# Retention followed by a gated cosine MLP: the order of the opening blocks, of the weight and block loads, and of the transposes against the stores

## The chip, the cores and the metric

The kernel runs on one core of a Trainium2 chip. The metric is the device time in microseconds (us) of one execution. Three runs of the kernel before gave 314.37, 314.63 and 315.67 us, so the median is 314.63 us. A profiled execution, from which every duration below comes, took 315.27 us; its span from the first to the last instruction was 313.6 us, and 1.7 us lie around the span.

Engines carry the profile's names: PE (TensorE matmul), PEld (its weight loads), DVE (VectorE), ACT (ScalarE), POOL (GpSimd) and SP (SyncE, which here only issues transfers). A name with q (SPq, POOLq) is the sequencer of that engine.

## The reference

Two layers follow each other. The first is a retention: for 8 batches and 8 heads, q, k and v have 576 rows of 64 numbers.

```python
scores = scale * np.matmul(q, k.transpose(0, 1, 3, 2))
Dmat = np.where(rel >= 0, gamma[:, None, None] ** rel[None, :, :], 0.0)
ret = scores * Dmat[None, :, :, :]
attn_out = np.matmul(ret, v)
```

The output is laid out as x with 4608 tokens of 512 numbers, and the second layer is

```python
h = x @ w_in            # 512 -> 2048
g = h * np.cos(h)
out = g @ w_out         # 2048 -> 512
```

## The kernel before

**Tiles.** The 4608 tokens are cut into 18 blocks of 256 (number j), and two blocks make a stage of 512 tokens (number n, 0 to 8). The retention of a block is computed in chunks of 128 tokens with a state that is carried from chunk to chunk.

**One block of retention.** `load` (L134 for pairs of rows, L148 for the later blocks) fetches q, k and v on SP's queue into buffers of which there are three for each name (`AHEAD = 3`). `scaled` (L165) multiplies q and k with the decay and rounds them into `qks`; `round_v` (L176, with L180 to L183 for chunks that cross the end of a batch) rounds v into `vb`. The transpose to `qkT` is done on PE for blocks 0 to 3 (`transpose_pe`, L209, with an evacuation of PSUM at L214) and by a DMA transpose on SP's queue for later ones (`transpose_dma`, L196). `scores` (L238, L267) multiplies, and a mask on DVE gives `ret` (L247, L277). `scores_y` (L299, L307) is the same in halves, for block 3. `sums_of` (L331) gives the chunk's own state; DVE adds it to the running one (L348 to L361) and ACT rounds it into `sb` (L371). `out_own` (L387) and `out_carried` (L419) accumulate the block's output in one PSUM tile `ov`, which is evacuated as `xT` (L442, or L444 on ACT and L445 on DVE in halves).

**The layers of a stage.** `mm1` (L457) makes eight blocks of h, each 1024 numbers wide in PSUM: 16 matmuls of 256 columns in stages 0 and 1, and 8 of 512 in the others. ACT takes the cosine (L465, a sine with a bias of half pi), and DVE multiplies it with h into `gT` (L466). The second layer of stage 0 is 64 plain matmuls (L865) with other work inserted after given numbers of them (the list `todo`). From stage 1 on it is a product of the Strassen kind: seven products (L557) of sums of quarters of g (`g_sum`, L504, on DVE and, for sum 7 from stage 2 on, on POOL) and of w_out (`w_sums`, L484), put together in `ot` (L583, L587) and stored (`stored_rows`, L573, on SP's queue).

**Order.** It is written out by hand (`manual_schedule`): each engine runs its instructions in the order of the program, and SP and POOL issue transfers in that order too. A transfer of a later line can't overtake an instruction that waits ahead of it on the same queue. `load_w_in` and `load_w_out` (L657, L663) are issued on POOL, in four pieces each. `load(..., gate=x)` makes the first transfer of a block wait until the weight transfer x has landed. In the kernel before, block 2 waits for the first piece of w_out (`w_dma[4]`), and block 3 for the third (`w_dma[6]`). `step` prepares the next block: four `scaled` on POOL, the DMA transpose, `round_v`, and the load of one more block; `steps_to(j)` does so until block j-1 is prepared. `stored(u)`, called after store u of a stage, calls it:

```python
if n == 1:
    steps_to({3: 7}.get(u, 0))
elif n == 2:
    steps_to({0: 8, 1: 9, 2: 10, 3: 11}[u])
else:
    steps_to({0: 2 * n + 6, 1: 2 * n + 7}.get(u, 0))
```

**PSUM.** There are three tags of two banks, a, b and m, and two of one, n and st. The blocks of stage 0 take them in the order m, b, m, a, b, m, a, b (`banks_of`); a block waits until the tile that had its tag before has been read.

Of the kernel before, what the change touches and what calls it, by code (L numbers as in the profile page):

```python
# [8 lines left out]
F32 = mybir.dt.float32  # L9
# [3 lines left out]
ACTF = mybir.ActivationFunctionType  # L13
# [4 lines left out]
def kernel(  # L18
# [51 lines left out]
    lng = consts.tile([P, H], F32)  # L70
    ln_scale = consts.tile([P, 1], F32)
    half_pi = consts.tile([P, 1], F32)
    qpos_i = consts.tile([P, PERQ, 2, H], I32)
    qpos = consts.tile([P, PERQ, 2, H], F32)
    kpos_i = consts.tile([P, PERK, H], I32)
# [354 lines left out]
    def x_of(j):  # L430
        n = j // 2
        if ("x", n) not in tiles:
            tiles["x", n] = xp.tile([P, DG, W], BF16, tag="xT", name="xT")
        return tiles["x", n][:, :, j % 2 * BK : j % 2 * BK + BK]
# [12 lines left out]
    def mm1(n, et, c0, w, bank, inside={}):  # L447
        if ("g", n) not in tiles:
            tiles["g", n] = gp.tile([P, ET, W], BF16, tag="gT", name="gT")
        gT, xT = tiles["g", n], tiles["x", n]  # L450
        m = 1024 // w
        ps = psum.tile([P, m, w], F32, tag=bank, name="h")
        for j in range(m):
            if j in inside:
                inside[j]()
            for dg in range(DG):
                nc.tensor.matmul(  # L457
                    ps[:, j, :],
                    lhsT=w_in_sb[:, dg, (et + j) * P : (et + j + 1) * P],
                    rhs=xT[:, dg, c0 : c0 + w],  # L460
                    start=(dg == 0),
                    stop=(dg == DG - 1),
                )
        cosh = cosp.tile([P, m, w], F32, tag="cosh", name="cosh")
        nc.scalar.activation(cosh, ps, ACTF.Sin, bias=half_pi, scale=1.0)  # L465
        nc.vector.tensor_mul(gT[:, et : et + m, c0 : c0 + w], ps, cosh)  # L466
# [169 lines left out]
    def load_next(**kw):  # L636
        nonlocal loaded
        if loaded < NB:
            load(loaded, **kw)
            loaded += 1  # L640
# [15 lines left out]
    def load_w_in(e0):  # L656
        return nc.gpsimd.dma_start(  # L657
            w_in_sb[:, :, e0 : e0 + 512],
            moe_w_in[:, e0 : e0 + 512].rearrange("(dg p) e -> p dg e", p=P),
        )  # L660
# [80 lines left out]
    scaled(nc.vector, 0, "q", 1)  # L741
    transpose_pe(0, "q", "n", act, (0,))
    transpose_pe(0, "q", "st", vec, (1,))
    round_v(0)
    w_dma = [load_w_in(0)]
    scaled(nc.gpsimd, 1, "k", 0)
    scaled(nc.gpsimd, 1, "k", 1)
    w_dma += [load_w_in(512)]
    for masked in scores(0, "ab", idle=2):
        masked()  # L750
    sums_of(0, "st")()()
    scaled(nc.vector, 1, "q", 0)
    scaled(nc.vector, 1, "q", 1)
    transpose_pe(1, "k", "n", act, (0,))
    ps0 = psum.tile([P, DG, BK], F32, tag="m", name="ov")
    out_own(0, ps0)
    transpose_pe(1, "k", "st", act, (1,))
    out_carried(0, ps0)
    act(x_of(0)[:, :2], ps0[:, :2])
    vec(x_of(0)[:, 2:], ps0[:, 2:])  # L760
    transpose_pe(1, "q", "n", act, (0,))
    transpose_pe(1, "q", "st", vec, (1,))
    round_v(1)
    w_dma += [load_w_in(e) for e in (1024, 1536)] + [load_w_out(0)]
    m1 = scores(1, "ab", idle=2)
    m1[0]()
    add1 = sums_of(1, "st")
    m1[1]()
    add1()()
    load_next(names="kqv", gate=w_dma[4])  # L770
    nc.gpsimd.tensor_copy(mask_mix, mask_p)
    nc.gpsimd.tensor_copy(mask_cmix, mask_c)
    for r in range(2):
# [3 lines left out]
    for name in "kq":  # L777
        for y in range(2):
            scaled(nc.gpsimd, 2, name, y)
        w_dma += [load_w_out(4 + "kq".index(name) * 4)]  # L780
    round_v(2)
    w_dma += [load_w_out(12)]
    load_next(names="kqv", gate=w_dma[6])
    load_next()
    prep(3)
    round_v(3)
# [19 lines left out]
    blocks_of[0][1:3] = blocks_of[0][2:0:-1]  # L806
    banks_of = {0: "mbmabmab", 1: "abmamabm"}

    later = {}

    def block2_scores():
        masks = scores(2, "ab")
        masks[0]()
        add = sums_of(2, "a")
        masks[1]()
        add()()

    def block3_sums():
        sums_of(3, "n")()()
# [1 line left out]
    for n in range(NT):  # L821
        blocks = blocks_of.get(n) or [(e + k * E2, 0, W) for e in range(0, E2, 2) for k in range(2)]
        for i, (et, c0, cw) in enumerate(blocks):
            inside = {
                (0, 0): {2: lambda: outputs(1, "a", act, vec)},
                (1, 1): {1: lambda: scores_y(3, 0, ("n", "st"))},
                (1, 2): {1: lambda: scores_y(3, 1, ("n", "st"))},
                (1, 3): {2: block3_sums},
            }.get((n, i), {})
            mm1(n, et, c0, cw, banks_of.get(n, "abmabmab")[i], inside)  # L830
            if (n, i) == (1, 1):
                steps_to(5)
            if (n, i) == (1, 3):
                outputs(3, "b", act, vec)
                for e in range(0, E2, 2):
                    w_sums(7, e, e + 2)
            if (n, i) == (1, 5):
                steps_to(6)
            if n:
                sums_after(n, i)  # L840
        if n == 0:
            gT = tiles["g", n]
            two = psum.tile([P, 2, DM], F32, tag="m", name="o")
            pss = [psum.tile([P, DM], F32, tag=t, name="o") for t in ("n", "st")]
            pss += [two[:, k] for k in range(2)]
            todo = [
                (12, lambda: transpose_pe(2, "k", "a", act)),
                (18, lambda: transpose_pe(2, "q", "b", act)),
                (26, block2_scores),
                (46, lambda: outputs(2, "b", act, vec)),  # L850
                (56, lambda: transpose_pe(3, "k", "a", act)),
                (62, lambda: transpose_pe(3, "q", "b", act)),
            ]
            todo += [
                (at, lambda x=x, e=e: w_sums(x, e, e + 4))
                for at, x, e in (
                    (4, 5, 0), (10, 5, 4), (50, 6, 0), (53, 6, 4), (57, 4, 0), (60, 4, 4)
                )
            ]
            todo.sort(key=lambda u: u[0])  # L860
            for done in range(4 * ET):
                while todo and todo[0][0] <= done:
                    todo.pop(0)[1]()
                e, t = divmod(done, 4)
                nc.tensor.matmul(  # L865
                    pss[t],
                    lhsT=gT[:, e, t * P : (t + 1) * P],
                    rhs=w_out_sb[:, e, :],
                    start=(e == 0),
                    stop=(e == ET - 1),  # L870
                )
            for t in range(4):
                ot = op.tile([P, 1, DM], F32, tag="abcd"[t], name="ot")
                (act, vec)[t % 2](ot[:, 0], pss[t])
                stored_rows(t * P, 0, DM, ot)
            load_next()
            load_next()
            continue

        a, b = 2 * n + 2, 2 * n + 3  # L880

        def first_unit(flush, pend):
            def then():
                late_sums(n, (5, 6))
                flush()
                outputs(a, "m")

            intro(b, "ab", "st", pend, then)

        def second_unit(flush, pend):  # L890
            def then():
                flush()
                outputs(b, "m")

            if b + 1 < NB:
                intro(b + 1, "ab", "st", pend, then)
            else:
                then()

        def only_intro(flush, pend):  # L900
            flush()
            if n == 1:
                late_sums(n, (7,))
            intro(a, "ab", "m")
            if n == 1:
                pend.append(lambda: late_sums(n, (3,)))

        def mid_unit(flush, pend):
            def then():
                flush()  # L910
                outputs(a, "m")

            intro(b, "ab", "st", pend, then)

        def end_unit(flush, pend):
            def then():
                flush()
                outputs(b, "m")

            if n > 1:  # L920
                intro(b + 1, "ba", "a", pend, then)
            else:
                then()

        if n in (1, 2):
            at = {6: only_intro, 5: mid_unit, 3: end_unit}
        else:
            at = {2: first_unit, 5: second_unit} if n < last else {}

        def stored(u):  # L930
            if n == 1:
                steps_to({3: 7}.get(u, 0))
            elif n == 2:
                steps_to({0: 8, 1: 9, 2: 10, 3: 11}[u])
            else:
                steps_to({0: 2 * n + 6, 1: 2 * n + 7}.get(u, 0))

        mm2_seven(n, at, stored)


# [28 lines left out]
```

## Time and profile before

| what | value |
|---|---|
| median of 3 runs | 314.63 us |
| profiled execution | 315.27 us |
| its span | 313.6 us |
| PE busy | 288.6 us (92%) |
| DVE busy | 220.1 us (70%) |
| POOL busy | 152.6 us (49%) |
| ACT busy | 136.3 us (43%) |
| mean granted clock of PE | 0.966 |
| PE idle for anything it waited for, after 136 us | none |

In the timeline a row has its start, its duration, the engine, the source line, the operation with output and inputs, and the number of instructions; in brackets stands the idle time of the engine ahead of it and what ended it. In the chain of waits each row is a piece of the chain that ended last. In the list of waits a row has the waiting line, what it waited for, the sum in us, the number of waits and the longest. In the windows a row has its stretch, its length, the busy time of PE, PEld, DVE, ACT and POOL (with instructions), the granted clock of PE (1.00 is full), the busy share of the DMA engines and the rate in GB/s.

### The profile page before, as it was taken

What the parts mean: (1) busy time and instruction counts of PE and PEld (TensorE: products, weight loads), DVE (VectorE), ACT (ScalarE), POOL (GpSimd) and SP (SyncE); (2) the same over time, 40 slices, a digit from 0 to 9 for tenths busy, and PEclk for the clock granted to TensorE, in tenths of its full rate; (3) what the DMA queues carried; (4) which work ended last, traced back from release to release, by engine and by line L of the source; (5) the groups of instructions that cost most, each with busy time, mean ns of one, the idle gap of its engine ahead of it and who ended that gap; (6) DMA issues with size and microseconds to landing.
All of it is one profiled execution on the core that took longest, in us unless ns stands there. A gap on an engine that the chain in (4) does not pass through costs nothing.

```text
span 313.6 us, 7653 instructions
## 1 busy us (share of the span) xinstructions
PE 288.6 (92%) x3258; PEld 197.4 (63%) x3258; DVE 220.1 (70%) x270; ACT 136.3 (43%) x158; POOL 152.6 (49%) x182
## 2 busy tenths in 40 slices
PE   7787989869999997599999999999999999999991
PEld 3566745758874585344884587468648855874680
DVE  5755754856985997349965977797689669836931
ACT  3535532544344623046435633663364446326520
POOL 7910936996301399813972493269247113102300
PEclk9799999998999999589999999999999999999997
DMA  7996989999998829999999819964700530121014
GB/s 228 275 190 162 167 154 270 225 221 243 243 255 199 202 65 248 239 186 278 208 246 214 203 40 239 249 148 103 167 3 2 119 84 0 36 69 35 2 33 100
DMA packets 128930, 49.78 MB, mean 159 GB/s; under 512 B 89344, under 2 KB 128384, under 8 KB 128896
## 3 DMA queue, kind: packets, MB, share of 16 engines
q1 hardware_dynamic: 124672, 45.10, 60.5%
q0 software_dynamic: 4224, 4.19, 8.6%
q8 instruction: 25, 0.41, 0.5%
q14 instruction: 9, 0.07, 0.1%
HBM read 36.70 MB, written 9.44 MB: 147 GB/s over the span
## 4 chain that ended last, share of the span: by engine, by line
PE 70%; DMA 9%; POOL 8%; DVE 5%; issue 3%; ACT 1%; SPq 1%; DVEq 0%; POOLq 0%; ACTq 0%
PE h L457 33%; PE o L557 28%; POOL qks L165 4%; DMA w_out_sb<-in_moe_w_out_dram 4%; DMA fk<-in_k_dram 3%; PE o L865 3%; DVE gT L466 2%; DMA fv<-in_v_dram 2%; PE ov L387 2%; PE sc L267 2%; PE st L331 1%; ACT cosh L465 1%; POOL vb L176 1%; DMA qkT<-qks 1%; PE ov L419 1%
## 5 line engine op out<-in xcount | busy, mean ns | idle before, releaser
L457 PE MATMUL h<-xT,w_in_sb 128*128 128x512 bf16 (+1 forms) x704 | 129.8, 345 | 3.8 <-DVE gT L466 1.6
L466 DVE TENSOR_TENSOR gT<-h,cosh 128x1024 bf16<-128x1024 f32 x72 | 87.9, 1222 | 39.0 <-ACT cosh L465 38.8
L465 ACT ACTIVATE cosh<-h,half_pi 128x1024 f32<-128x1024 f32 x72 | 80.1, 1114 | 79.7 <-PE h L457 79.7
L457 PEld LDWEIGHTS <-w_in_sb 128*128 128x128 bf16 x704 | 69.6, 99 | 60.4 <-issue 5.2
L504 POOL TENSOR_TENSOR gs<-gT 128x512 bf16<-128x512 bf16 x28 | 35.8, 1279 | 116.6 <-DVE gT L466 116.6
L557 PEld LDWEIGHTS <-gs 128*128 128x128 bf16 x520 | 50.2, 99 | 7.3 <-issue 0.2
L557 PEld LDWEIGHTS <-gT 128*128 128x128 bf16 x384 | 37.1, 98 | 6.2
L165 POOL TENSOR_TENSOR qks<-fq,gq 128x512 bf16<-128x512 f32 x32 | 35.5, 1131 | 3.2 <-DMA fq<-in_q_dram 3.1
L583 DVE TENSOR_TENSOR ot<-ot,o 128x512 f32<-128x512 f32 x39 | 25.9, 680 | 14.0 <-ACT ot L587 7.9
L587 ACT COPY ot<-o 128x512 f32<-128x512 f32 x32 | 18.7, 586 | 38.7 <-PE o L557 38.7
L277 DVE TENSOR_TENSOR ret<-sc,mask_c 128x1024 bf16<-128x1024 f32 x25 | 29.8, 1213 | 4.8 <-PE sc L267 4.8
L557 PE MATMUL o<-w_out_sb,gs 128*128 128x256 bf16 (+1 forms) x264 | 32.3, 278 | 0.0
L165 POOL TENSOR_TENSOR qks<-fk,gkc 128x512 bf16<-128x512 f32 x28 | 31.3, 1137 | 0.0
L557 PE MATMUL o<-ws,gs 128*128 128x256 bf16 x256 | 30.7, 273 | 0.0
L557 PE MATMUL o<-w_out_sb,gT 128*128 128x256 bf16 x256 | 30.1, 273 | 0.0
L176 POOL CAST vb<-fv 128x512 bf16<-128x512 f32 x36 | 22.5, 653 | 1.4 <-DMA fv<-in_v_dram 1.4
L442 ACT CAST xT<-ov 128x1024 bf16<-128x1024 f32 x14 | 14.2, 1012 | 12.2 <-PE ov L419 12.2
L371 ACT CAST sb<-s 128x512 bf16<-128x512 f32 (+1 forms) x18 | 10.3, 574 | 18.2 <-DVE s L359 7.7
L387 PE MATMUL ov<-ret,vb 128*64 128x128 bf16 (+1 forms) x352 | 12.9, 229 | 3.9 <-DVE ret L277 1.9
L165 POOL TENSOR_TENSOR qks<-fk,gkp 128x512 bf16<-128x512 f32 x6 | 6.1, 1043 | 21.0 <-DMA fk<-in_k_dram 20.9
L361 DVE TENSOR_TENSOR s<-st,s 128x256 f32<-128x256 f32 x18 | 7.6, 423 | 11.7 <-PE st L331 11.4
L504 DVE TENSOR_TENSOR gs<-gT 128x512 bf16<-128x512 bf16 (+1 forms) x25 | 15.4, 615 | 0.4
(81 smaller groups left out, 216.8 us busy)
## 6 DMA issues: line engine op xcount, KB each, us to landing
out_dram<-ot SPq DMA_DIRECT2D x70, 128.0 KB, 2.5
fk<-in_k_dram SPq DMA_DIRECT2D x25, 256.0 KB, 4.8
fv<-in_v_dram SPq DMA_DIRECT2D x25, 256.0 KB, 4.6
fq<-in_q_dram SPq DMA_DIRECT2D x12, 512.0 KB, 4.3
w_in_sb<-in_moe_w_in_dram POOLq DMA_DIRECT2D x4, 512.0 KB, 6.9
w_out_sb<-in_moe_w_out_dram POOLq DMA_DIRECT2D x4, 512.0 KB, 6.4
fk<-in_k_dram SPq DMA_DIRECT2D x3, 512.0 KB, 6.0
fv<-in_v_dram SPq DMA_DIRECT2D x3, 512.0 KB, 6.0
```

What stands on the lines that cost most here:

```text
L165: return eng.tensor_tensor(out=dst.rearrange("p b a d -> p a b d"), in0=src.rearrange("p (a b) d -> p a b d", a=2), in1=by.rearrange("p (a ...
L176: runs[y](vb[:, y], f[:, :, y, :] if j < NP_B else f[:, y])
L277: nc.vector.tensor_tensor(out=ret[:, k].rearrange("p a b i -> p (a b) i"), in0=pss[k].rearrange("p a b i -> p (a b) i"), in1=mask.unsqueez ...
L387: nc.tensor.matmul(ps[h % 2 * D : h % 2 * D + D, h // 2, c.c0 : c.c0 + P], lhsT=vb[c.rows, y, h, :], rhs=rhs, start=part not in begun, sto ...
L442: evac(x, ps)
L457: nc.tensor.matmul(ps[:, j, :], lhsT=w_in_sb[:, dg, (et + j) * P : (et + j + 1) * P], rhs=xT[:, dg, c0 : c0 + w], start=(dg == 0), stop=(d ...
L465: nc.scalar.activation(cosh, ps, ACTF.Sin, bias=half_pi, scale=1.0)
L466: nc.vector.tensor_mul(gT[:, et : et + m, c0 : c0 + w], ps, cosh)
L504: eng.tensor_tensor(out=tiles["gs", n, x][:, e : e + step], in0=a[:, e : e + step], in1=b[:, e : e + step], op=op_,)
L557: nc.tensor.matmul(dst[i], lhsT=lhs[:, e, j * P : (j + 1) * P], rhs=rhs[:, e, c0:c1], start=(fresh and e == 0 and (i == 0 or len(parts) > 2)),
L583: return lambda: nc.vector.tensor_tensor(out=out_, in0=in0, in1=in1, op=ALU.add)
L587: nc.scalar.copy(t, tiles["all", x])
```

## The change

The change only moves work, with two additions: a sine of one number for each partition, and one constant tile for its result.

1. **Opening, blocks 0 and 1.** One half of v of block 0 is rounded on ACT in place of POOL, and both halves of block 1 too. The scaling of half 0 of q of block 1 goes from DVE to POOL, ahead of the second to fourth pieces of w_in. The evacuations of three transposes of block 1 go from ACT to DVE. `xT` of block 0 is evacuated by ACT alone. The scores of block 1 lose the two warming matmuls ahead of them, and both masks come after the state sums. The tiny sine is issued on ACT ahead of the scores.
2. **Block 1's output.** `outputs(1)` stood inside the first block of layer one. Now `out_own(1)` comes behind that whole block, `out_carried(1)` after a quarter of the second block, and ACT evacuates it ahead of the second block's cosine.
3. **Weights and loads.** The first two pieces of w_out are issued straight after w_in. Block 2's loads wait for the fourth piece of w_in, and block 3's for the second piece of w_out.
4. **Second layer of stage 0.** Block 2's scores come after 24 matmuls (26 before) and its state sums after 34, no longer straight behind the scores. Block 3's transposes come after 52 and 59 (56 and 62 before). `outputs(2)` and `outputs(3)` are evacuated by ACT alone.
5. **Steps.** One of the two loads behind stage 0 goes. Block 4 is prepared after block (1, 0) of layer one, block 5 after (1, 4), block 6 after store 0 of stage 1, block 7 after store 3, and block 8 after block (2, 2) of layer one, ahead of POOL's sums of stage 2. On SP's queue the transposes of blocks 4 to 8 so stand ahead of loads and stores that they stood behind.

```diff
+        if (n, et, c0) == (0, 4, 0):
+            nc.scalar.copy(x_of(1), ps1[0])
         cosh = cosp.tile([P, m, w], F32, tag="cosh", name="cosh")
...
-    round_v(0)
+    round_v(0, (nc.gpsimd.tensor_copy, act))
     w_dma = [load_w_in(0)]
-    scaled(nc.gpsimd, 1, "k", 0)
-    scaled(nc.gpsimd, 1, "k", 1)
-    w_dma += [load_w_in(512)]
     for masked in scores(0, "ab", idle=2):
         masked()
     sums_of(0, "st")()()
-    scaled(nc.vector, 1, "q", 0)
+    scaled(nc.gpsimd, 1, "k", 0)
+    transpose_pe(1, "k", "n", act, (0,))
+    scaled(nc.gpsimd, 1, "k", 1)
+    scaled(nc.gpsimd, 1, "q", 0)
     scaled(nc.vector, 1, "q", 1)
-    transpose_pe(1, "k", "n", act, (0,))
+    w_dma += [load_w_in(e) for e in (512, 1024, 1536)] + [load_w_out(e) for e in (0, 4)]
+    load_next(names="kqv", gate=w_dma[3])
+    round_v(1, (act, act))
     ps0 = psum.tile([P, DG, BK], F32, tag="m", name="ov")
     out_own(0, ps0)
-    transpose_pe(1, "k", "st", act, (1,))
+    transpose_pe(1, "k", "st", vec, (1,))
     out_carried(0, ps0)
-    act(x_of(0)[:, :2], ps0[:, :2])
-    vec(x_of(0)[:, 2:], ps0[:, 2:])
-    transpose_pe(1, "q", "n", act, (0,))
+    act(x_of(0), ps0)
+    transpose_pe(1, "q", "n", vec, (0,))
     transpose_pe(1, "q", "st", vec, (1,))
-    round_v(1)
-    w_dma += [load_w_in(e) for e in (1024, 1536)] + [load_w_out(0)]
-    m1 = scores(1, "ab", idle=2)
-    m1[0]()
+    nc.scalar.activation(sine, half_pi, ACTF.Sin, bias=0.0, scale=1.0)
+    masks1 = scores(1, "ab")
     add1 = sums_of(1, "st")
-    m1[1]()
+    for masked in masks1:
+        masked()
     add1()()
-    load_next(names="kqv", gate=w_dma[4])
...
-        w_dma += [load_w_out(4 + "kq".index(name) * 4)]
+        w_dma += [load_w_out(8 + "kq".index(name) * 4)]
     round_v(2)
-    w_dma += [load_w_out(12)]
-    load_next(names="kqv", gate=w_dma[6])
+    load_next(names="kqv", gate=w_dma[5])
     load_next()
...
-                (0, 0): {2: lambda: outputs(1, "a", act, vec)},
+                (0, 1): {1: block1_carried},
...
-            if (n, i) == (1, 1):
+            if (n, i) == (0, 0):
+                block1_own()
+            if (n, i) == (1, 0):
                 steps_to(5)
             if (n, i) == (1, 3):
-                outputs(3, "b", act, vec)
+                outputs(3, "b")
...
-            if (n, i) == (1, 5):
+            if (n, i) == (1, 4):
                 steps_to(6)
+            if (n, i) == (2, 2):
+                steps_to(9)
...
-                (26, block2_scores),
-                (46, lambda: outputs(2, "b", act, vec)),
-                (56, lambda: transpose_pe(3, "k", "a", act)),
-                (62, lambda: transpose_pe(3, "q", "b", act)),
+                (24, block2_scores),
+                (34, block2_sums),
+                (46, lambda: outputs(2, "b")),
+                (52, lambda: transpose_pe(3, "k", "a", act)),
+                (59, lambda: transpose_pe(3, "q", "b", act)),
...
             load_next()
-            load_next()
...
             if n == 1:
-                steps_to({3: 7}.get(u, 0))
-            elif n == 2:
-                steps_to({0: 8, 1: 9, 2: 10, 3: 11}[u])
+                steps_to({0: 7, 3: 8}.get(u, 0))
             else:
-                steps_to({0: 2 * n + 6, 1: 2 * n + 7}.get(u, 0))
+                steps_to({0: 2 * n + 6, 2: 2 * n + 7}.get(u, 0))
```

The new helpers `block1_own` and `block1_carried` call `out_own(1)` into a PSUM tile of tag a and `out_carried(1)` into the same; `block2_sums` calls `sums_of(2, "a")`.

## Prediction

> **What bounds the kernel now.** I read the list of PE's waits first, because PE is busy 92% of the span and after 136 us waits for nothing at all. Every time that a change of order can win therefore lies ahead of that point, in waits of PE and in the clock that PE loses through them. (Better than 0.5%, some 1.6 us, is what a measurement of this kernel can tell from no change.) PE's waits in the whole span, those that matter here:
>
> ```profile
> PE sc L267 <- DMA qkT<-qks: 4.5, 1, 4.5
> PE ov L387 <- DVE ret L277: 1.9, 2, 1.4
> PE h L457 <- DVE gT L466: 1.6, 1, 1.6
> ...
> PE st L331 <- DVE ret L247: 1.4, 1, 1.4
> ...
> PE h L457 <- ACT xT L444: 1.1, 1, 1.1
> PE h L457 <- DVE xT L445: 1.0, 1, 1.0
> ```
>
> Then the windows, cut where the granted clock changes (the columns are length, busy PE, PEld, DVE, ACT, POOL, clock, DMA share, GB/s):
>
> ```profile
> 22.78:26.19 3.41, 1.76 (x17) 1.44 (x15) 2.00 (x2) 2.37 (x3) 0.00 (x0) 1.00 0.91 150
> ...
> 67.15:70.56 3.41, 1.34 (x10) 1.02 (x10) 1.82 (x2) 1.01 (x2) 3.41 (x5) 0.95 0.84 189
> 70.56:73.97 3.41, 3.41 (x19) 2.45 (x18) 0.58 (x1) 1.11 (x1) 1.01 (x2) 0.54 1.06 258
> ...
> 121.76:125.17 3.41, 1.38 (x42) 0.94 (x40) 2.75 (x4) 0.55 (x1) 3.41 (x5) 0.96 1.06 240
> 125.17:135.41 10.24, 6.33 (x54) 4.00 (x55) 3.04 (x3) 0.76 (x2) 7.05 (x9) 0.51 0.98 232
> ```
>
> A stretch of 3.4 us with 1.34 or 1.38 us of PE work is followed by half the clock, for 3.4 us and for 10.2 us; one with 1.76 us of work is not. So a wait costs itself and, past a point between these, half of the PE work that follows. Last, the chain of waits up to the longest of them:
>
> ```profile
> 109.39 0.19 POOL gs L504
> ...
> 111.62 3.67 POOL qks L165 x3
> ...
> 117.90 4.06 DMA fk<-in_k_dram
> 121.96 3.20 POOL qks L165 x4
> 125.16 3.88 DMA qkT<-qks
> ...
> 129.08 1.07 PE sc L267 x29
> ```
>
> POOL's sums of g (L504) hold up the preparation of block 7, whose transpose stands ahead of block 10's load and block 8's transpose on SP's queue; PE waits for that last one from 124.6 to 129.1 us.
>
> **Step 1, the opening: -2.8 us.** In the timeline, block (0, 0) of layer one does 8 matmuls at 17.58 us and then PE waits 0.85 us for block 1's mask and 0.24 us for `sb`. Its cosine comes only at 23.04 us, behind half an `xT` (21.14 us, 0.59 us) and the table load:
>
> ```profile
> 21.74 1.28 ACT L465 ACT_TABLE_LOAD   x1
> 23.04 2.12 ACT L465 ACTIVATE cosh<-h,half_pi 128x1024 f32<-128x1024 f32 x2
> 24.18 2.35 DVE L466 TENSOR_TENSOR gT<-h,cosh 128x1024 bf16<-128x1024 f32 x2 [1.73 <-ACT cosh L465]
> 25.46 1.25 PE L457 MATMUL h<-xT,w_in_sb 128*128 128x256 bf16 x10 [1.65 <-DVE gT L466]
> ```
>
> The third block starts at 25.46 us, when `gT` has freed bank m. After the change I lay the same rows in the new order. POOL: half of v (0.59), the issue of w_in (0.95), then three `qks` of 1.02 each end at about 12.6. DVE: masks of block 0 to 12.2, one `qks` of 1.24, three evacuations of 0.42 as PE delivers them, the last at about 15.8. Scores of block 1 at 16.0 (16.39 before), masks (2.35) to 19.0, state add (0.68) to 19.7, `sb` (0.62) to 20.3. On PE, state sums (0.8) and all 16 matmuls of (0, 0) fill 16.6 to 19.0, then own, a quarter of (0, 1), carried at 20.35, the rest until 22.0. On ACT, in its order: `sb` to 20.3, cosine (1.11) to 21.4, `xT` of block 1 (1.01, row L442) to 22.4; the table load (1.28) ran at about 15.6 to 16.9, where ACT waits for `sb`. DVE's `gT` (1.23) ends at 22.7, and the third block starts there: 25.5 - 22.7 = 2.8 us. The w_in piece for block (0, 1) landed at 12.05 + 6.4 = 18.45 us; it is issued 0.55 us later now, and even 19.0 is ahead of its use at 19.7 (if not, the wait is the excess). Block 1's v on ACT needs `fv`, landed at 12.4, and costs 2 x 0.6 ahead of `xT` of block 0 at 14.5: covered. The six blocks that follow take 10.5 us as before, at PE's pace.
>
> **Step 2, weights and loads: 0.** Second piece of w_out: five pieces landed 2.5 to 3.0 us apart on the same queue, so a sixth lands at about 26.55 + 2.6 = 29.2 us when alone; it is used at about 36.5. Block 2's load is gated 2.5 us earlier (24.05 for 26.55). Even if sharing gives that back, POOL's rows of before (k ready at 33.6, q at 36.4, `v_mix` at 41.7) meet PE's new wants (35.7, 37.4, 41.8). Block 3's load starts at 29 to 33 us (41.8 before); its k and q, ready at 50.9 and 54.2 before, are wanted at 47.7 and 49.5, so 5 of the 9 us are needed. The third and fourth pieces of w_out landed at 41.8 and 48.6; wanted at 41.5 and 46.9. They are issued behind two `scaled` each, 3 to 7 us earlier, and now meet loads 3 and 4. Ends: nothing, or what rival B says. I take nothing, the nearest row being the 7.0 us (5.5 to 5.7 without) of the piece that met load 3 before.
>
> The Trainium skill (DMA: Bandwidth & Descriptors, "Issuing engines are not separate DMA queues") says that transfers of all issuing engines interleave on the same 16 DMA engines. By that, early loads would slow the weights, and this part could cost rather than be free; the 7.0 us beside 5.5 is the only trace of it here, and by it the sum would lose 1.5 us at most if a piece had no slack.
>
> **Step 3, second layer of stage 0: -1.4 us.** State sums straight behind the scores took bank a and waited 1.37 us for the mask. Ten matmuls of 0.21 us now stand between, 2.1 us, with two masks of 1.2 us: the first has freed the bank. The layer took 35.94 to 55.5; it now runs from about 33.1 to 51.3.
>
> **Step 4, block 3's output: -0.6 us, and -1.7 us of clock.** PE waited 1.13 us for ACT's half of `xT` and 1.00 for DVE's, which stood behind `gT`. One evacuation by ACT (1.01) behind the cosine that ends at 67.69 gives 68.7: 62 matmuls start at 68.97 for 69.60. PE now works about 3.41 - 1.66 = 1.75 us of that stretch; the row with 1.76 kept the clock, the one with 1.34 lost it. I take the nearer: 3.41 / 2 = 1.7 us are not lost.
>
> The Trainium skill (TensorE: Matmul & The Clock Gate, "HAM oscillation") allows PE gaps up to 3.4 us. The trace differs: the clock fell after waits of 1.13 and 1.00 us. By the rule the clock is safe in the new order with more to spare; by the row it is close. Both give the same 1.7 us, with different certainty.
>
> **Step 5, transposes ahead: -4.5 us, and -3.1 us of clock.** I walk SP's queue with durations of before: eight stores of block 0 (5.1) from about 51.9; load 5 (6.2) to 63.2; transpose 4 (2.4); load 6 (6.9) to 72.5; transpose 5 (3.0); load 7 (5.7) to 81; two store halves (1.3), transpose 6 (2.5), load 8 (5.9) to 91, landed at 95; six stores (5), transpose 7 at 96, load 9 (5), transpose 8 at 103, landed at 107. Wanted, in the new time: transpose 4 at 75 (lands 69), 5 at 82 (79), 6 at 105.6 (88), 7 at 112.8 (102), 8 at 118. So the 4.5 us go with 11 us to spare. POOL prepares 4 at once behind 3, so its queue carries them: block 8 from 91 to 97 (four of 1.13, two of 0.65, the last behind the landing). Behind that stand the sums of g, four of 1.28, wanted by product 7 at 116.35 - 6.5 = 109.8: ready at about 103. Six stores behind load 8 free their `ot` tiles at about 97, wanted again at 104. What is late next is PE itself, and the 1.4 us wait for `ret` at 123.8, which stays; a stretch with it alone has some 2 us of work, above 1.76. So the 10.24 us at half clock, of which 6.3 were PE work, give back 3.1 us.
>
> **Sum.** 2.8 + 1.4 + 0.6 + 1.7 + 4.5 + 3.1 = 14.1 us. The profiled execution took 315.27 us, so 301.2 us. It lies 0.64 us above the median of the runs, which are 1.3 us apart; by the median it would be 300.5. I keep **301.2**.
>
> **Rivals.**
> - *A, clock not won.* The cold stretch of step 4 stays (1.7), or one more comes in the opening, whose two warming matmuls (0.77 us at 15.3) are gone (1.7). For it: 1.75 us is at the edge. Against: 1.76 kept the clock. 302.9 to 304.6.
> - *B, weights late.* Loads 3 and 4 push the last pieces of w_out behind them. Begun at 31 us, the two loads (1.57 MB each, 4.5 us at the 346 GB/s of the first loads, some 6 for the later, small rows) and the two pieces (2.6 each, three with interference) would end at 47 to 49; the last 16 matmuls and inserts (5 us) then end at 54.5 where 51.3 was hoped for, with up to 1.7 of clock: 3 to 5 us, 304 to 306.
> - *C, the transpose isn't won.* Block 8's load or POOL is late enough that PE waits as before. Only steps 1, 3 and 4 remain: 315.27 - 6.5 = 308.8. Against: 11 us of slack.
> - *D, slower.* On POOL, block 8's preparation now stands ahead of the sums of g. If load 8 lands at t, the sums end at about t + 8, and product 7 waits from t = 102 on, 1 us for each us, plus half clock. From t = 116 on, the gain of 14 is eaten: 317 and more. Against: load 8 landed at about 96.5 even in the old order.
>
> **How the numbers follow.** Forecast 0.58, A 0.17, B 0.10, C 0.07, D 0.05, better by up to 2 us 0.03 (PE's two waits at 60 us, 0.8, and most of the 1.66 of step 4 go too: 299.0). The range 299.0 to 306.0 holds all but C and D, somewhat over 8 in 10. Faster: all but D and a part of the unknown, 0.92; same 0.02; slower 0.06.
>
> **What would show it.** Step 1: third block of L457 near 22.7 us, the table load before 18 us. Step 2: no wait of L865 for w_out. Step 3: no wait of L331 for `ret`. Step 4: one wait of L457 for `xT`, below 1.7 us, full clock behind it. Step 5: no wait of L267 for a DMA, and full clock from the opening to the end. Wrong, if PE waits for w_out or for `gs`, or if the clock falls at a place where it did not before.

## The result, and the profile after

The changed kernel takes 314.17 us (median of 17 runs, 309.97 to 318.22) where the kernel before took 315.25 beside it: a ratio of 0.993, with a 95% interval of 0.990 to 0.996. Here and below, times are medians of all runs, while ratios leave out the slow runs, those over 1.5% above the fastest of their kernel (7 of these 17, the profiled one among them, and 2 of the 4 of e9). The forecast was 301.2 with a range from 299.0 to 306.0, so it was wrong by 13 us, and the time lies outside the range. The profiled execution took 315.17 us (span 313.5), 0.1 less than that of before. A second profile of the same kernel, of 314.48 us (e1 below), shows the same waits, each longer or shorter by up to 1 us, and is given where it matters.

The lines of the changed kernel are numbered 1 to 13 higher: L457 of before is L458, L557 is L560, L865 is L878. PE's waits, to be laid beside the list of before:

```profile
PE o L560 <- POOL qks L166: 3.4, 1, 3.4
PE o L878 <- DMA w_out_sb<-in_moe_w_out_dram: 2.2, 1, 2.2
PE tr L210 <- POOL qks L166: 2.1, 3, 1.2
PE ov L388 <- DVE ret L278: 1.9, 2, 1.4
...
PE h L458 <- ACT xT L443: 1.6, 1, 1.6
```

Every wait that the change was aimed at is gone: 4.5 us of L267 for a transpose, 1.6 of L457 for `gT`, 1.4 of L331 for `ret`, and the two for halves of `xT` have become one. But new ones stand in their place, for w_out, for `qks`, and one of 3.4 us in the second layer. The start of each stage on PE tells where the gain was won and given back:

| start of | before | forecast | after |
|---|---|---|---|
| second layer, stage 0 | 35.94 | 33.1 | 33.01 |
| first layer, stage 1 | 55.56 | 51.3 | 56.49 |
| first layer, stage 2 | 94.50 | 88.0 | 95.08 |
| first layer, stage 3 | 133.47 | 119.4 | 128.90 |
| first layer, stage 4 | 163.65 | 149.6 | 163.50 |

(Forecasts are those of before less the terms due by then: 94.50 - 6.5, and from stage 3 on less 14.1.) The opening came out to 0.1 us as forecast. All of it was lost in the second layer of stage 0; 4.6 us were won by stage 3, and lost again in the next 35.

**The first loss.** The chain of waits of after there:

```profile
25.98 7.85 DMA fk<-in_k_dram
...
33.97 1.99 POOL qks L166 x2
35.96 9.16 DMA w_out_sb<-in_moe_w_out_dram
...
45.16 0.59 PE o L878 x2
```

Block 2's k takes 7.85 us to land (4.44 before, at 26.94), so POOL is later with `qks`, and the third piece of w_out, issued behind it, takes 9.16 us. PE waits 2.17 us for it and then works at half clock for 3.4 us. In the second profile the wait is 1.5 us, and the clock stays.

**The second loss.** The timeline of after, at the end of stage 2 (brackets hold the wait of the engine and what ended it):

```profile
149.96 3.21 SPq L576 DMA_DIRECT2D out_dram<-ot  x4
...
154.38 1.07 ACT L590 COPY ot<-o 128x512 f32<-128x512 f32 x2 [6.99 <-DMA out_dram<-ot]
155.01 3.35 PE L560 MATMUL o<-w_out_sb,gs 128*128 128x256 bf16 x15 [3.42 <-POOL qks L166]
```

The list of waits names `qks`, but the product at 155.01 needs a PSUM bank that ACT's copy at 154.38 reads, and that copy waited 7 us for a store to free its `ot` tile. The store stood on SP's queue behind a transpose and a load. The two stretches that follow (PE busy is the first number after the length):

```profile
151.60:155.01 3.41, 0.00 (x0) 0.00 (x0) 0.00 (x0) 0.63 (x2) 3.33 (x5) 1.00 0.91 210
155.01:158.42 3.41, 3.40 (x16) 2.16 (x15) 0.00 (x0) 0.44 (x1) 2.13 (x4) 0.50 0.94 201
```

A stretch without any PE work, then one at half clock: 3.4 us and 1.7.

**What both have in common** is that transfers are slower, and this is so from the start, before the order differs. The line of the DMA queue on the page (packets, MB, time of the packets as a share of 16 engines' span), of before:

```profile
q1 hardware_dynamic: 124672, 45.10, 60.5%
```

and of after:

```profile
q1 hardware_dynamic: 124672, 45.10, 74.0%
```

The same packets and bytes take 0.605 x 16 x 313.6 / 124672 = 24.4 ns each before, and 29.8 ns after. In the first 8 us, where both kernels load blocks 0 and 1 in the same order and nothing else (the first weights are issued at 9.1 us), the windows give 231 GB/s before and 208 after (206 in the second profile). Loads of 256 KB (k) landed in 4.8 us at the median before and in 5.5 after, transposes in 4.0 and 5.0.

### The profile page after: what moved, and what is told of

Its sections match the earlier page's. It is cut to its first block, busy times and chain, and to the rows that moved or that the text cites. A ratio compares the mean times of both kernels' runs of the same rounds, so it can differ in the third digit from the quotient of the medians.

```text
span 313.5 us, 7628 instructions
## 1 busy us (share of the span) xinstructions
PE 287.7 (92%) x3256; PEld 195.6 (62%) x3256; DVE 217.9 (70%) x267; ACT 139.0 (44%) x160; POOL 151.7 (48%) x180
## 3 DMA queue, kind: packets, MB, share of 16 engines
q1 hardware_dynamic: 124672, 45.10, 74.0%
## 4 chain that ended last, share of the span: by engine, by line
PE 66%; DMA 11%; DVE 10%; POOL 6%; issue 2%; ACT 2%; SPq 1%; DVEq 0%; POOLq 0%; ACTq 0%
PE h L458 29%; PE o L560 27%; DMA fk<-in_k_dram 5%; DVE gT L469 4%; POOL qks L166 4%; DMA w_in_sb<-in_moe_w_in_dram 3%; DMA w_out_sb<-in_moe_w_out_dram 3%; DVE gs L507 3%; PE o L878 3%; PE ov L388 2%; PE st L332 2%; ACT cosh L468 2%; DVE ret L278 2%; PE sc L268 1%; PE ov L420 1%
## 5 line engine op out<-in xcount | busy, mean ns | idle before, releaser
L458 PE MATMUL h<-xT,w_in_sb 128*128 128x512 bf16 (+1 forms) x704 | 128.8, 344 | 3.0 <-ACT xT L443 1.6
L469 DVE TENSOR_TENSOR gT<-h,cosh 128x1024 bf16<-128x1024 f32 x72 | 88.0, 1222 | 40.3 <-ACT cosh L468 40.1
L458 PEld LDWEIGHTS <-w_in_sb 128*128 128x128 bf16 x704 | 69.2, 99 | 58.9 <-issue 1.5
L560 PEld LDWEIGHTS <-gs 128*128 128x128 bf16 x520 | 50.0, 99 | 11.3 <-issue 3.6
L166 POOL TENSOR_TENSOR qks<-fq,gq 128x512 bf16<-128x512 f32 x33 | 36.4, 1122 | 21.9 <-DMA fq<-in_q_dram 21.7
L560 PEld LDWEIGHTS <-gT 128*128 128x128 bf16 x384 | 37.1, 98 | 7.6 <-DVE gT L469 1.4
L590 ACT COPY ot<-o 128x512 f32<-128x512 f32 x32 | 18.7, 587 | 45.3 <-PE o L560 36.5
L560 PE MATMUL o<-w_out_sb,gs 128*128 128x256 bf16 (+1 forms) x264 | 32.2, 278 | 3.4 <-POOL qks L166 3.4
L560 PE MATMUL o<-w_out_sb,gT 128*128 128x256 bf16 x256 | 30.3, 273 | 1.1 <-DVE gT L469 1.1
L560 PE MATMUL o<-ws,gs 128*128 128x256 bf16 x256 | 30.8, 273 | 0.2 <-DVE gs L507 0.2
L278 DVE TENSOR_TENSOR ret<-sc,mask_c 128x1024 bf16<-128x1024 f32 x25 | 29.8, 1215 | 0.0
L177 POOL CAST vb<-fv 128x512 bf16<-128x512 f32 x33 | 21.5, 669 | 7.7 <-DMA fv<-in_v_dram 7.4
L443 ACT CAST xT<-ov 128x1024 bf16<-128x1024 f32 x16 | 16.2, 1012 | 15.6 <-PE ov L420 15.6
L362 DVE TENSOR_TENSOR s<-st,s 128x256 f32<-128x256 f32 x18 | 7.6, 423 | 17.2 <-PE st L332 16.8
L372 ACT CAST sb<-s 128x512 bf16<-128x512 f32 (+1 forms) x18 | 10.3, 575 | 18.7 <-DVE s L360 8.0
L878 PE MATMUL o<-w_out_sb,gT 128*128 128x512 bf16 x64 | 16.5, 401 | 2.2 <-DMA w_out_sb<-in_moe_w_out_dram 2.2
L507 DVE TENSOR_TENSOR gs<-gs,gT 128x1024 bf16<-128x1024 bf16 x16 | 15.8, 986 | 0.3
L560 PE MATMUL o<-ws,gT 128*128 128x256 bf16 x128 | 15.3, 272 | 0.0
```

Source lines behind the costliest of these rows:

```text
L166: return eng.tensor_tensor(out=dst.rearrange("p b a d -> p a b d"), in0=src.rearrange("p (a b) d -> p a b d", a=2), in1=by.rearrange("p (a ...
L177: runs[y](vb[:, y], f[:, :, y, :] if j < NP_B else f[:, y])
L278: nc.vector.tensor_tensor(out=ret[:, k].rearrange("p a b i -> p (a b) i"), in0=pss[k].rearrange("p a b i -> p (a b) i"), in1=mask.unsqueez ...
L443: evac(x, ps)
L458: nc.tensor.matmul(ps[:, j, :], lhsT=w_in_sb[:, dg, (et + j) * P : (et + j + 1) * P], rhs=xT[:, dg, c0 : c0 + w], start=(dg == 0), stop=(d ...
L507: eng.tensor_tensor(out=tiles["gs", n, x][:, e : e + step], in0=a[:, e : e + step], in1=b[:, e : e + step], op=op_,)
```

## The experiments

I first held that the order alone does it (earlier loads beside the weights; transposes and loads ahead of the stores), against the rival that one execution was slow by chance.

**e1**, after unchanged.

> The changed kernel as it is, for a second profile. Theory 1 (the order itself makes the new waits): the first 57 us again hold a wait of the second layer of stage 0 for a piece of w_out, 2 us or more, and stage 3 again a wait of 3 us or more of product 7, whose bank waits for the copy of u1, whose ot tile waits for a store that stands behind a transpose and a load on SP's queue; time 310 to 315. Theory 2 (that one execution moved its data slowly: its first 8 us ran at 208 GB/s where the kernel before had 231): with 230 GB/s in the first 8 us both waits are below 0.5 us and the time is 301 to 304.

313.32 us, 0.994 [0.991, 0.997]: 206 GB/s in the first 8 us, a share of 74.1%, and the wait for `qks` (that is, for the `ot` tile) again, of 4.4 us. The wait for w_out is 1.5 us, below the 2 that were expected. The slow transfers are not chance.

**e2**, before with step 5 alone (the new places of `steps_to`, and one load less behind stage 0), and **e3**, after with the old ones, so all but step 5:

```diff
-            if (n, i) == (1, 1):
+            if (n, i) == (1, 0):
                 steps_to(5)
...
-            if (n, i) == (1, 5):
+            if (n, i) == (1, 4):
                 steps_to(6)
+            if (n, i) == (2, 2):
+                steps_to(9)
...
-            load_next()
...
-                steps_to({3: 7}.get(u, 0))
-            elif n == 2:
-                steps_to({0: 8, 1: 9, 2: 10, 3: 11}[u])
+                steps_to({0: 7, 3: 8}.get(u, 0))
             else:
-                steps_to({0: 2 * n + 6, 1: 2 * n + 7}.get(u, 0))
+                steps_to({0: 2 * n + 6, 2: 2 * n + 7}.get(u, 0))
```

(e3 is the reverse of it, made on after.)

> The kernel before with the new places of the steps alone (step 5), its opening unchanged. Theory 1: the 4.5 us wait for block 8's transpose and 3.1 us of clock go, but the wait for the ot tile in stage 3 comes (3.4 us and up to 1.7 of clock): 3 us faster, 311 to 313. Theory 2, and the forecast's step 5: 7.6 us faster, 307 to 308, and no wait in stage 3.

> The changed kernel with the old places of the steps: steps 1 to 4 of the forecast alone. Theory 1: the second layer of stage 0 starts near 33 us and ends near 55 to 57, since it waits for block 2's qks and for w_out; the wait for block 8's transpose stays: 314 to 317. Theory 2, and the forecast: it ends near 51.5 us, 6.5 us faster, 308 to 309.

e2: 308.55 us, 0.980 [0.977, 0.984], 234 GB/s. e3: 322.07 us, 1.022 [1.016, 1.028], 210 GB/s. Step 5 gives 5.9 us by itself (314.43 for before beside it), and the rest of the change costs 7.6, though every wait that it aimed at in the opening is gone. It is 210 or 234 GB/s in the first 8 us, where e2 and e3 load the same blocks in the same order. So neither theory holds: step 5 wins without a new wait, and the opening alone loses.

**e4**, after with two buffers for three of the four `ot` tiles, so that a late store holds up nobody.

```diff
-    op = ctx.enter_context(tc.tile_pool(name="op", bufs=1))
+    op1 = ctx.enter_context(tc.tile_pool(name="op", bufs=1))
+    op2 = ctx.enter_context(tc.tile_pool(name="op2", bufs=2))
+    op = {"a": op1, "b": op2, "c": op2, "d": op2}
...
-            t = op.tile([P, 2, N2], F32, tag=tag, name="ot")
+            t = op[tag].tile([P, 2, N2], F32, tag=tag, name="ot")
...
```

> The changed kernel with two buffers each for the ot tiles b, c and d, so that the copy of u1 need not wait for the store of the stage before. Theory 1: the wait in stage 3 goes and with it 3.4 us and up to 1.7 us of clock against the changed kernel of the same call: 306 to 310. Rival (the wait is for POOL, as the list of waits names it): the wait stays, same time as the changed kernel.

308.19 us, 0.980 [0.974, 0.986]; the wait of 3.4 us is gone. So the reading of the second loss holds: it was the `ot` tile. The transfers are as slow as in after (209 GB/s, 75.1%): it cures what they cause.

What after, e1, e3 and e4 share and before and e2 lack is the new constant tile `sine`, one number for each partition. In the compiled programs (no profile prints their addresses; the distances agree with the sizes of the tiles) it takes 32 bytes of every partition, and all tiles declared behind it move by 32: `w_in_sb` from 27392 to 27424, the first `fk` from 72448 to 72480. All of these were multiples of 256 before, and none is after. That made a third theory: **the transfers are slower because their addresses in SBUF are off the multiples of 256 bytes.** The rival stayed the order, in which a moved address changes nothing.

**e5** is after with 256 bytes for the tile, and **e6** is e3 with the same:

```diff
-    sine = consts.tile([P, 1], F32)
+    sine = consts.tile([P, 64], F32)
...
-    nc.scalar.activation(sine, half_pi, ACTF.Sin, bias=0.0, scale=1.0)
+    nc.scalar.activation(sine[:, :1], half_pi, ACTF.Sin, bias=0.0, scale=1.0)
```

**e7** and **e8** are before with a tile that nothing reads, of 32 and of 128 bytes (`[P, 32]`):

```diff
     half_pi = consts.tile([P, 1], F32)
+    pad = consts.tile([P, 8], F32)
...
+    nc.vector.memset(pad[:, :1], 0.0)
```

> The changed kernel with the tile sine 256 bytes wide in place of 4, of which one number is used. All later tiles of a partition then begin, as in the kernel before, at multiples of 256 bytes; with the 4-byte tile they began 32 bytes off. Theory 3 (the loads of both kinds, whose rows are 256 and 512 bytes, and the DMA transposes are slower into addresses that are 32 bytes off): the first 8 us run at 230 GB/s, block 2's k lands by 31 us, the wait for w_out and the one in stage 3 are below 0.5 us, and the time is 301 to 304. Theory 1 (the order of the transfers alone): 310 to 315 as before. Theory 2 (chance): no change beyond the spread.

> The opening alone (old places of the steps), with the tile sine 256 bytes wide. Theory 3: the second layer of stage 0 ends near 51.5 us in place of 55.6, and the time is 308 to 311 in place of 322. Theory 1: 317 to 322.

> The kernel before with one unused tile of 32 bytes at the place of sine and a write of one number into it (0.06 us of DVE); nothing else. Theory 3: the first 8 us fall from 231 to about 208 GB/s, block 8's transpose comes later than before, and the time is 318 to 326. Theories 1 and 2: 314 to 316.

> The same with an unused tile of 128 bytes: all later tiles begin 128 bytes past a multiple of 256. If the boundary that counts is 256 bytes, the rate falls as with 32 bytes and the time with it (318 to 326); if it is 64 or 128 bytes, both are as in the kernel before (314 to 316).

e5: 304.25 us, 0.964 [0.957, 0.970], 233 GB/s. e6: 310.41 us, 0.985 [0.977, 0.992], 230 GB/s. e7: 325.82 us, 1.035 [1.025, 1.045], 207 GB/s. e8: 324.64 us, 1.026 [1.018, 1.034], 209 GB/s. A tile that nothing reads makes the kernel before 2.6 to 3.5% slower, and the change with 252 idle bytes more is 10 us faster than after (304.25 for 314.17). The order as the cause of the slow transfers falls. e5 came a little worse than expected: 304.25 us for at most 304, block 2's k at 32.3 us for 31, and a wait for w_out of 0.84 us for less than 0.5.

**e9** and **e10** split the tiles. In e9 the pad of 32 bytes stands behind `w_out_sb`: the weights keep their places, the buffers of q, k, v, `qkT` and `ot` are off. In e10, 32 bytes stand ahead of the weights and 224 behind them: only the weights and the constants are off. **e11** is the control, e7 with 256 bytes.

```diff
     half_pi = consts.tile([P, 1], F32)
+    pad = consts.tile([P, 8], F32)
...
     w_out_sb = consts.tile([P, ET, DM], BF16)
+    pad2 = consts.tile([P, 56], F32)
```

(This is e10; e9 has `pad` in the place of `pad2`; e11 has `pad` alone, with 64 numbers.)

> The kernel before, with an unused tile of 32 bytes for each partition declared behind the two weight tiles: the weights keep their addresses (multiples of 256 bytes), the loads of q, k and v, the transposed tiles and the output tiles move by 32. Theory (the transfers of loads, transposes and stores suffer, in proportion to their bytes): 1.02 to 1.04 of before, 208 to 212 GB/s in the first 8 us, the queue's share 68% or more. Rival (it is the weights, or the operands of PE, that suffer): 0.995 to 1.005, 230 GB/s, 60 to 63%.

> The kernel before, with 32 bytes ahead of the weights and 224 behind them: the weights and the constants ahead of them stand off by 32, all loads, transposed tiles and output tiles stand at multiples of 256 again. Theory: 230 GB/s in the first 8 us, the queue's share 60 to 64%, 1.00 to 1.01 of before (4 MB of 45 are weights, landing somewhat later). Rival (weights decide): 1.02 to 1.04.

> A control: the kernel before, with an unused tile of 256 bytes in the place where e7 and e8 had 32 and 128. Everything moves by 256 and stays at multiples of 256. Theory (the boundary of 256 bytes decides): 0.995 to 1.005 of before, 230 GB/s in the first 8 us, share 60 to 63%. Rival (any new tile or any moved address changes the time): 1.02 to 1.04 as with 32 and 128.

e9: 328.1 us, 1.031 [1.022, 1.040], 203 GB/s. e10: 315.34 us, 1.000 [0.996, 1.004], 231 GB/s. e11: 315.15 us, 0.997 [0.994, 1.000], 230 GB/s. The queue's line on the page of e9:

```profile
q1 hardware_dynamic: 124672, 45.10, 70.2%
```

and of e10, with the line of the weights' queue below it:

```profile
q1 hardware_dynamic: 124672, 45.10, 60.3%
q0 software_dynamic: 4224, 4.19, 8.5%
```

It is the addresses behind the weights that count; a tile moved by 256 costs nothing, and the weights may stand off. The operands of the engines move there too, but their instructions take the same (before and e9: mask 1213 and 1215 ns, `xT` 1012 and 1012, `gT` 1222 and 1221), so it is the transfers. In the old order their price shows as four waits for a transpose, 11.4 us in e9, where before has one of 4.5.

Loads pay by themselves: in the first 8 us no other transfers run, and e9 moves 203 GB/s for 231. Stores hardly pay: 128 KB land in 2.6 us for 2.5. Transposes land in 4.5 us for 4.0 and k of 256 KB in 5.7 for 4.8, but they share the queue, and no run has transposes alone off.

The design as a table, ratio to before:

| order | aligned | off by 32 |
|---|---|---|
| before | 1 (e11, 256 off: 0.997) | 1.035 (e7) |
| all but step 5 | 0.985 (e6) | 1.022 (e3) |
| the whole change | 0.964 (e5) | 0.993 (after) |

The order is worth 3.6% aligned and 4% (0.993 / 1.035) off; the tile costs 3 to 4% under every order.

**e12**, e5 with block 3's load gated by the fourth piece of w_out (`gate=w_dma[7]` for `w_dma[5]`), for what is left of rival B.

> The aligned changed kernel (e5), with block 3's loads gated by the fourth piece of w_out in place of the second. If rival B of the prediction took part (loads 2 and 3 delay the last pieces of w_out): the wait of L878 for w_out (0.84 us) goes, the second layer of stage 0 ends 0.8 to 1 us sooner than 52.23, and the time is 303 to 304. If block 3's load is then late itself, PE waits for its k or q near 47 us instead and the time is 304 to 306.

305.67 us, 0.966 [0.959, 0.973]: the intervals of e5 and e12 overlap almost wholly. The wait for w_out is gone and the second layer of stage 0 takes 18.29 us (35.17 to 53.46) for 19.84 in e5. But it began 2.8 us later in this profile, behind half the clock from 11.9 to 22.2 us, ahead of anything that the gate touches. e6, which keeps the old gate, has no such wait either and takes 18.28 us (33.99 to 52.27), as PE comes 1.6 us later than in e5. In e12 the third piece of w_out lands 5.8 us after its issue, 7.83 in e5; whether this helps the kernel the time does not tell.

## Why the prediction was wrong, point by point

**The step that failed** is one without a term: the new tile. The list of the change names "one constant tile for its result", and the sum puts what it moves at nothing, without a reason. Steps 2 and 5 then take transfer times from rows of before ("I walk SP's queue with durations of before"), and those no longer held: a packet took 29.8 ns for 24.4. That is 10 of the 13 us (314.17 for after, 304.25 for e5).

What was right and wrong beside it is read from e5, the change without that cost. PE's waits of e5:

```profile
PE ov L388 <- DVE ret L278: 2.0, 2, 1.4
PE h L458 <- ACT xT L443: 1.6, 1, 1.6
...
PE tr L210 <- POOL qks L166: 1.0, 2, 0.7
PE o L878 <- DMA w_out_sb<-in_moe_w_out_dram: 0.8, 1, 0.8
```

- **Step 1 (-2.8) was right in its mechanism; its size came out with luck.** The second layer of stage 0 starts at 33.01 us in after and 32.39 in e5 (33.1 forecast), and the table load is at 16.06 in after, as laid out. But the seven profiles with the new opening start it at 32.39 to 35.46, the seven with the old one at 35.31 to 36.69: 33.8 and 36.0 on the mean, so 2.2 us. The clock differs among them: after has full clock there, e12 half clock from 11.9 to 22.2 us. No term of step 1 allows for that; rival A does.
- **Step 2 (0) was wrong in e5** by one wait of 0.84 us, and right in e6, where PE comes later. The early load 2 slows itself and the weights: in e5 `fk` of block 2 lands in 8.17 us (4.44 before) and the third piece of w_out in 7.83. So k's 7.85 us in after come from the order, not from the address. This is rival B's mechanism at about a quarter of its price; off the boundary the same wait is 1.5 to 2.2 in after, e1 and e4.
- **Step 3 (-1.4) was right**: the wait of L331 for `ret` is in neither list. The layer takes 18.28 us in e6 and 19.84 in e5 (18.2 forecast), and 0.84 of the 1.6 between them is the wait for w_out.
- **Step 4 (-0.6, clock -1.7) was right where the clock stayed.** One wait of 1.55 us is left, below 1.7 as forecast. The first layer of stage 1 takes 22.47 us before, 20.07 in e6 (2.4 won, 2.3 forecast), and 21.73 in e5, where the clock fell. That is rival A, and the reason can be read from the traces. In each of them the stretches at half clock begin whole multiples of 3.41 us from one another (before at 12.22, 70.25 and 124.86: 17 and 16 times; e5 at 14.19 and 65.39: 15 times; e6 at 12.30 and 121.53: 32 times), but at other places in every execution. Cut at e5's own places:

```profile
61.98:65.39 3.41, 1.57 (x52) 0.97 (x51) 1.71 (x3) 2.54 (x3) 3.04 (x3) 1.00 1.17 264
65.39:68.80 3.41, 3.41 (x17) 2.37 (x17) 0.23 (x1) 0.00 (x0) 2.21 (x3) 0.50 0.94 169
```

  and at those of e6, where the same wait of 1.55 us ends at 65.36 (65.31 in e5):

```profile
63.50:66.91 3.41, 1.86 (x27) 1.62 (x28) 1.22 (x1) 1.80 (x2) 3.39 (x4) 1.00 0.85 195
66.91:70.32 3.41, 3.41 (x34) 3.06 (x32) 1.78 (x2) 2.23 (x2) 1.78 (x4) 1.00 1.12 276
```

  The wait is the same, but e5's stretch ends with it and holds 1.57 us of work, and e6's begins just ahead of it and holds 1.86. The changed kernel itself shows both: 1.57 and half clock in after, 1.86 and full clock in e1. So these pairs do not refute the reading that 1.34 us of work lose the clock and 1.76 keep it (between 1.6 and 2.2 both happen, see the end). What the prediction had wrong is that it laid one stretch round the wait (1.75 us), as if its place were given; which way it falls is luck.
- **Step 5 (-4.5, clock -3.1) was right in size**, where the transfers keep their times: e2, with that step alone, gives 5.9 us of 7.6, and e5 gains 6.4 us between the starts of stages 2 and 3 (94.50 - 91.53 = 3.0, then 133.47 - 124.07 = 9.4). Between the starts of stages 2 and 4, e2 and e5 both gain 7.2 us: the half clock of before ran on to 135.1 us, into stage 3. No wait of L268 for a DMA is left in either kernel. In after, "what is late next is PE itself" was wrong: the store of `ot` was, behind a transpose and a load that now stand ahead of it and are slower. The walk looked at the stores of stage 1 (free at 97, wanted at 104) and not at those of stage 2.

With the addresses kept, 304.25 us would have been inside the range. In profiled executions e5 is 3.9 us behind the forecast (305.07 for 301.2), and the starts of the stages share it out: 0.7 better in the opening, 1.6 worse in the second layer of stage 0, 2.6 in stage 1, 1.1 in stage 2, and 0.8 better in stage 3 (29.4 us for 30.2). The last two are mostly one thing: the table books all of step 5 to stage 2, while before lost 0.8 us of it in stage 3 (its first layer there took 14.79 us, 13.99 in e5). Of stage 1's 2.6, 1.7 are the clock; its second layer takes 17.57 us for 16.47 before, with new waits of 0.53 us for DVE's state (L362) and 0.23 for `gT`, and what makes DVE later stays open. None of the rivals as priced was the case for after: no rival named the tile. Rival A's price (302.9 to 304.6) holds e5.

## What to carry to other kernels

A line that declares a tile moves all tiles behind it. Compare the SBUF addresses of the transfers before and after a change, and pad a small constant to 256 bytes. (To declare it behind the weights, as the pad of e9 is, does not help: the buffers of the loads still stand behind it.) When a profile after a change shows the same packets and bytes at a higher share of the DMA engines, and the rate differs in a stretch where both kernels do the same, look for what changed in the transfers themselves before looking at the order.

## What the runs showed of the hardware

- **Transfers of short rows are slower at SBUF addresses 32 or 128 bytes off a multiple of 256.** Aligned, the first 8 us move 229 to 234 GB/s (before, e2, e5, e6, e10, e11, e12), off by 32 or 128 they move 203 to 210 (after, e1, e3, e4, e7, e8, e9). The mean packet takes 24.1 to 24.6 ns for 28.4 to 29.8. The traces hold every packet, and by size the means are: 256 bytes (loads of single rows, transposes) 18.7 to 19.5 ns aligned and 23.7 to 25.2 off; 512 bytes (loads of two rows) 29.5 to 30.7 and 32.3 to 34.2; 1024 bytes (stores) 60.7 to 64.3 and 65.4 to 67.0. The weights' packets of 1024 bytes show nothing (104 ns before, 103 in e10).
- The Trainium skill (DMA: Bandwidth & Descriptors, "How a descriptor splits into AXI transactions") says that a transaction can read less than 256 bytes but has to start at a multiple of 256, so that the first one of a piece that begins elsewhere starts at the boundary below it. An estimate from this: a row of 256 bytes off the boundary takes two transactions for one, and by the page's beats of 32 bytes 9 for 8 when 32 bytes off and 12 when 128 off. The runs agree that such rows are slower, for destinations too, but they make no difference between 32 and 128 bytes (23.8 and 23.7 ns for a packet of 256), so the beats do not explain it. Nor does a fixed price for each row: off by 32, 49% of these packets still take 18 ns or less (e9; 97% before), and the others more. How the time comes about stays open.
- **Whether a wait costs the clock depends on places 3.41 us apart that differ from execution to execution.** Cut at its own places, each of the 14 traces shows the same: all 23 stretches that began at full clock and held up to 1.6 us of PE work were followed by half the clock, and none with more than 2.2. Of 45 between, 13 were, ten of them in the first 18 us; what decides there stays open. A gain that is counted in clock is worth a chance, not a sum, unless the work clears that band.
